# A gated mix of a scan and an MLP on one core: tile 3 of B by transposing loads, a later gate product, half scan tables and carried states on GpSimd

## The chip, the core and the metric

The kernel runs on one core of a Trainium2 chip. The core has TensorE (PE; its weight loads are PEld), VectorE (DVE), ScalarE (ACT), GpSimd (POOL) and SyncE (SP), which here only issues DMAs. Transfers issued from SP and from POOL run on the same 16 DMA engines. The metric is the device time of one execution in microseconds (us), less is better.

## What is computed

```python
g = sigmoid((x * gate_w).sum(-1, keepdims=True))
# a: a diagonal complex recurrence over 2048 tokens, 1024 states
Bu   = einsum("bld,pd->blp", x, B_bar)        # B_bar from B_re, B_im, Lambda, dt
h[t] = Lam_bar * h[t-1] + Bu[t]
a    = 2 * einsum("blp,dp->bld", hseq, C).real + x * Dskip
# b: layer norm, then an MLP of 1024 -> 3584 -> 1024
b    = gelu(layernorm(x) @ w1 + b1) @ w2 + b2
out  = g * a + (1 - g) * b
```

x is 2048 x 1024, all inputs and the output are bfloat16.

## The kernel before

Everything is built as a graph of tasks (`Graph.add`, `Graph.dma`); `schedule` orders the tasks of each engine, and the kernel is then emitted in that order, with semaphore waits where a task needs another engine's result. PE's order is written out by hand (each product depends on the one before it). The order of ACT, DVE, POOL and SP is the planner's: `_latest` goes backwards from PE's order and gives each task a latest start, `_schedule_latest` goes forwards and lets each engine take the ready task with the earliest latest start. For a DMA the planner uses an issue time, a rate and a landing time (constants at the top of the file).

All large products are done in a form that needs seven products for a 2 x 2 block of tiles instead of eight (`SG`, steps p1 to p7; sums of the operands S1..S4, T1..T4 are made by DVE, partial sums are moved by ACT with `seed` and `snap`). One group of it in the first stage is 28 matmuls of 512 columns.

The stages:
- **Opening** (0 to about 28 us). x (rows 0 to 511) and the B rows of tiles 0 to 3 are loaded and transposed by PE (`t_x`, `t_b0`, `t_b`, 8 transposes for each 128 rows), and ACT or DVE copies the result from PSUM. Chunks 1 to 3 of x, 512 rows each, come by transposing loads of 1 MB (`xT_dma`, line 1232, SP). `bu_plain` makes the products of tile 0 with chunks 0 and 1, and the first steps of the groups of tiles 1 and 2 (`early`) stand between.
- **Products of x with B** (to about 112 us). Groups (tile, half of x) in the order (1,0), (2,0), (3,0), (0,1), (1,1), (2,1), (3,1), then tiles 4 to 7. Before p1 of a group, the B rows of its tile must be there with sums S1 to S4 (`b_sums`); T1 to T3 of a half of x are made in `x_sums`, T4 in `x_sum4`, which overwrites the place 2 of that half, where the first half of the odd chunk's transposed x stands. Tiles 4 to 7 come by transposing loads (`bT_dma`, line 1316). The gate product `z_gate` (line 1289: 32 matmuls with two columns of weights, needs all four chunks) stands inside group (2,0), ahead of its p6; its result goes to DRAM and back (`z_move`), and gives the gate and the sums for the layer norm. `ln_stats` squares x on ACT, works out mean and variance in small POOL instructions (lines 1253 to 1258), normalises on DVE and stores to DRAM; transposing loads (line 1468) bring it back for the MLP.
- **Scan tables** (lines 972 to about 1010). Powers of e^(i theta) for 256 positions of all eight tiles are made by doubling, 8 levels of 6 DVE instructions; the last level has 8 x 128 elements in a partition.
- **MLP**, with the scan as filler on DVE: 16 units (`ssm`), each with four products with tables and four combinations, eight scans of 256 positions (line 1426), and three small instructions (fx1, fx2, fx3: lines 1435, 1437, 1439) that turn the last states into the initial states of the next unit. The two temporary tiles MA and MB are shared by all units.
- **Product of the states with C** and the output (from about 451 us).

Of the kernel before, what the change touches and what calls it, by code (L numbers as in the profile page):

```python
# [17 lines left out]
DMA_LAT = 2.0  # L18
# [4 lines left out]
DMAT_BW = 150e3  # L23
OPENING = 12.0
SP_ISSUE = 0.12
ACT_ISSUE = 0.12
POOL_ISSUE = 1.2
# [144 lines left out]
class Graph:  # L172
# [7 lines left out]
    def add(self, eng, dur, prio, emit, reads=(), writes=(), name="", kind="c", nbytes=0, sem=None,  # L180
            xpose=False, extra=(), ndma=1, bw=None, thr=False):
        t = Task()
        t.bw = bw
# [41 lines left out]
    def _schedule_once(self):  # L225
# [27 lines left out]
        while ev:  # L253
# [17 lines left out]
            for e in engs:  # L271
# [25 lines left out]
                if t.kind == "dma":  # L297
                    issue_end = st + t.dur
                    push(issue_end, 1, e)
                    ts = max(issue_end, chan_free[e])  # L300
                    busy_o = sum(1 for o in chan_free if o != e and chan_free[o] > ts)
                    bw_eff = t.bw * (1.0, 0.55, 0.4)[busy_o]
# [78 lines left out]
    def _schedule_latest(self, ls):  # L381
# [57 lines left out]
        while ev:  # L439
# [8 lines left out]
            for e in engs:  # L448
# [13 lines left out]
                if t.kind == "dma":  # L462
                    issued = t.start + t.dur
                    push(issued, 1, e)
                    ts = max(issued, chan_free[e])
                    others = sum(1 for o in chan_free if o != e and chan_free[o] > ts)
                    chan_free[e] = ts + t.nbytes / (t.bw * (1.0, 0.55, 0.4)[others])
# [98 lines left out]
def build(nc, A_x, A_Lambda_re, A_Lambda_im, A_B_re, A_B_im, A_C_re, A_C_im, A_log_dt, A_Dskip,  # L566
# [25 lines left out]
    with es:  # L592
# [105 lines left out]
        for nm in ("DTC", "A", "TH", "R", "PHI", "KFX", "TTR", "T2", "KF2", "T3", "S1", "C1", "UR", "UI",  # L698
                   "Q", "Q2", "INV", "N1", "N2", "N3", "N4", "E20R", "E20I", "SS", "CC", "NMS"):
            alloc_cols(nm, PT)  # L700
# [163 lines left out]
        for pt in range(1, 4):  # L864
            load_b(pt, (-0.85, pt))
# [93 lines left out]
        def tmpd(which, n):  # L959
            return AR.v(TD + which * (PT * T // 2) * 4, [(n, PT), (1, n)], F32)  # L960
# [14 lines left out]
        v = w1(0, 0, 1)  # L975
        g.add("dve", 0.12, PT1, lambda e, v=v: e.memset(v.ap, 1.0), writes=[v], name="e1r0")
        v = w1(1, 0, 1)
        g.add("dve", 0.12, PT1, lambda e, v=v: e.memset(v.ap, 0.0), writes=[v], name="e1i0")
        for k in range(LT):
# [3 lines left out]
            a0, a1, o0, o1, t0, t1 = w1(0, 0, n), w1(1, 0, n), w1(0, n, n), w1(1, n, n), tmpd(0, n), tmpd(1, n)  # L983
# [6 lines left out]
        NTAB = PT * T  # L990
        e1r = AR.v(E1, [(T, PT), (1, T)], F32)
# [161 lines left out]
        def bu_plain(pt, c):  # L1153

            ks = 2
            for ri in range(2):
# [12 lines left out]
        def b_sums(pt, q):  # L1169
            def bv(i, dt=FP16):  # L1170
                return AR.v(bqo(pt, i), [(1, 512)], dt)
            dve_tt("bs1_%d" % pt, q, bv(4), bv(2, BF16), bv(3, BF16), ALU.add, 512)
            dve_tt("bs2_%d" % pt, q, bv(5), bv(4), bv(0, BF16), ALU.subtract, 512)
            dve_tt("bs3_%d" % pt, q, bv(6), bv(0, BF16), bv(2, BF16), ALU.subtract, 512)
# [9 lines left out]
        def x_sum4(pr, q):  # L1184
            xv2, xv1, xv5 = AR.v(xqo(pr, 2), [(1, 2048)], FP16), AR.v(xqo(pr, 1), [(1, 2048)]), AR.v(xqo(pr, 5), [(1, 2048)], FP16)
            dve_tt("ut4_%d" % pr, q, xv2, xv1, xv5, ALU.subtract, 2048)

        def bu_group(pt, pr):
# [8 lines left out]
            mv = {"B11": xl(0, BF16), "B21": xl(1, BF16), "B22": xl(3, BF16), "T1": xl(4), "T2": xl(5), "T3": xl(6), "T4": xl(2)}  # L1197
# [5 lines left out]
            uc = AR.v(SSM + 14336 if bu_n[0] < 7 else TD + 4096, [(1, 512)], F32)  # L1203
# [3 lines left out]
            def fin(qd, q, bk):  # L1207
# [6 lines left out]
                else:  # L1214
                    sv = su if ri == 0 else s5
                    src = sv
                    if ri == 0:
                        g.add("dve", c_dve(CH), (1.0, q - 2), lambda e: e.tensor_tensor(ev.ap, V(PS[bk], 0, [(1, 2 * T)]), src.ap, ALU.add),
                              reads=[b_ps[bk], sv], writes=[ev, b_ps[bk]], name="u" + nm)
# [10 lines left out]
        def xT_dma(c, prio):  # L1230
            o = AR.v(xqo(c // 2, 2 * (c % 2)), [(512, DT), (1, 512)])
            g.dma(prio, lambda e: e.dma_start_transpose(out=o.ap, in_=x2[c * CH:(c + 1) * CH, :]), CH * D * 2,  # L1232
                  ssem("xT", c), writes=[o], name="xT%d" % c, xpose=True, bw=240000.0)
# [79 lines left out]
        def bT_dma(pt):  # L1313
            for ri, ap in enumerate((A_B_re, A_B_im)):
                o = AR.v(bqo(pt, 2 * ri), [(128, DT), (1, 128)])
                g.dma((0.3, pt, ri), lambda e, o=o, ap=ap, pt=pt: e.dma_start_transpose(out=o.ap, in_=ap[pt * 128:(pt + 1) * 128, :]), 128 * D * 2,
                      ssem("bT", 2 * pt + ri), writes=[o], name="bTd%d.%d" % (pt, ri), xpose=True)
# [7 lines left out]
        t_b(3, (1.0, seq[0] + 0.5))  # L1325
        early[1].p2()
        bu_plain(0, 1)
# [8 lines left out]
        for n, (pt, pr) in enumerate(order):  # L1336
# [3 lines left out]
            if (pt, pr) == (0, 1):  # L1340
                x_sums(1, seq[0])
                x_sum4(1, seq[0])
# [8 lines left out]
            if n == 1:  # L1351
                z_gate()
                z_move()
                x_sum4(0, seq[0])
# [35 lines left out]
        def ssm(pg, q):  # L1390
# [37 lines left out]
            if q + 1 < NQ:  # L1428
# [6 lines left out]
                g.add("dve", 0.1, pri(20), lambda e: e.tensor_tensor(V(FXT, 8 * pg, [(2, 4), (1, 2)]), gsw.ap, V(CST, col["KF"] + 8 * pg, [(2, 4), (1, 2)]), ALU.mult),  # L1435
                      reads=[gsw, gfw, bc("KF")], writes=[b_fxt[pg]], name="fx1_" + tag)
                g.add("dve", 0.1, pri(61), lambda e: e.tensor_tensor(V(INIT, 8 * pg, [(2, 4), (1, 2)]), gfw.ap, V(CST, col[CTn] + 4 * pg, [(1, 4), (0, 2)]), ALU.mult),
                      reads=[gsw, gfw, bc(CTn)], writes=bi, name="fx2_" + tag)
                g.add("dve", 0.1, pri(62.5), lambda e: e.tensor_tensor(it, it, fx, ALU.add), reads=bi + [b_fxt[pg]], writes=bi, name="fx3_" + tag)
# [507 lines left out]
```

## Time and profile before

| | us |
|---|---|
| median of three runs | 551.88 |
| the three runs | 555.68, 551.75, 551.88 |
| the profiled execution, its own time | 554.73 |
| its span, first to last instruction | 553.0 |
| PE busy in the span | 546.1 (99%) |
| DVE busy | 510.2 (92%) |
| ACT busy | 287.1 (52%) |
| POOL busy | 89.7 (16%) |

The profile is of one execution. Times in its rows count from the start of the span. A busy PE is a modelled figure, as matmuls overlap; the start of the next row is the better measure of how long a step took.

### The profile page before, as it was taken

The numbers are of one execution on the slowest core, as the hardware profiler recorded it, in microseconds if no ns is written. First come the engines' busy times: TensorE is split into PE (matmuls) and PEld (weight loads), VectorE is DVE, ScalarE is ACT, GpSimd is POOL, SyncE is SP. The second block draws the span as 40 slices with busy tenths as digits, with TensorE's granted clock in tenths as the row PEclk, the third lists the DMA queues.
The fourth block names the chain that finished last, engine by engine and source line by source line (L and its number), as shares of the span: only waits on it lengthen the run. The fifth ranks groups of instructions, "written<-read, shape, count | busy, mean of one in ns | idle before, by whom it ended". The sixth has DMA issues, their size and how long they took to land.

```text
span 553.0 us, 7464 instructions
## 1 busy us (share of the span) xinstructions
PE 546.1 (99%) x2622; PEld 250.2 (45%) x2622; DVE 510.2 (92%) x880; ACT 287.1 (52%) x480; POOL 89.7 (16%) x146
## 2 busy tenths in 40 slices
PE   8899999999999999999999999999999999999997
PEld 5444444444444444444444444444444444444443
DVE  5879989999999999999999999999999999899863
ACT  3767887886773347773347762247672322111110
POOL 0127662540001010001110000220000111001000
PEclk9989999999999999999999999999999999999999
DMA  9996999789762455464666983797767999987531
GB/s 268 252 301 155 272 272 293 252 274 360 237 142 105 164 190 206 148 216 196 225 227 184 310 167 64 135 200 226 240 157 136 230 312 298 376 293 249 180 117 57
DMA packets 115054, 120.07 MB, mean 217 GB/s; under 512 B 70338, under 2 KB 92738, under 8 KB 113994
## 3 DMA queue, kind: packets, MB, share of 16 engines
q1 hardware_dynamic: 102400, 73.69, 47.9%
q0 software_dynamic: 12480, 45.90, 26.8%
q8 instruction: 20, 0.33, 0.2%
q14 instruction: 16, 0.13, 0.1%
q10 hardware_dynamic: 138, 0.02, 0.0%
HBM read 56.40 MB, written 47.46 MB: 188 GB/s over the span
## 4 chain that ended last, share of the span: by engine, by line
PE 94%; SPq 3%; DMA 2%; issue 0%; DVE 0%
PE ps L1034 71%; PE ps L1032 22%; SPq L1232 2%; DMA ar<-in_A_x_dram 2%; PE ps L1289 1%; PE ps L1100 0%; SPq L771 0%; SPq L784 0%; SPq L783 0%; SPq L857 0%; DVE ar L1732 0%
## 5 line engine op out<-in xcount | busy, mean ns | idle before, releaser
L1034 PE MATMUL ps<-ar 128*128 128x512 f16 (+1 forms) x1844 | 416.9, 379 | 0.0
L1034 PEld LDWEIGHTS ps<-ar 128*128 128x128 f16 (+1 forms) x1844 | 180.1, 98 | 218.1 <-issue 1.3
L1032 PE MATMUL ps<-ar 128*128 128x512 bf16 (+1 forms) x608 | 150.0, 379 | 0.0
L1119 DVE TENSOR_TENSOR ar<-ar 128x512 f16<-128x512 bf16 (+7 forms) x224 | 140.0, 662 | 3.9 <-PE ps L1289 2.0
L1032 PEld LDWEIGHTS ps<-ar 128*128 128x128 bf16 (+1 forms) x608 | 59.3, 98 | 71.5 <-ACT ar L833 0.4
L1426 DVE TENSOR_TENSOR_SCAN ar<-cst,init,ar 128x256 bf16<-128x256 f32 x128 | 88.1, 734 | 0.4
L1054 ACT ACTIVATE ar<-ps 128x512 f32<-128x512 f32 x102 | 59.8, 596 | 51.1 <-PE ps L1032 36.8
L1070 ACT ACTIVATE ps<-ps 128x512 f32<-128x512 f32 x67 | 39.0, 582 | 75.4 <-PE ps L1032 64.3
L1412 DVE TENSOR_TENSOR ar<-ar 128x2048 bf16<-128x2048 bf16 x64 | 77.0, 1217 | 0.2 <-ACT ar L1000 0.2
L1533 ACT ACTIVATE ar<-ps,cst 128x512 bf16<-128x512 f32 x56 | 38.4, 686 | 13.4 <-PE ps L1034 13.1
L1055 ACT ACTIVATE ar<-ps,cst 128x512 f32<-128x512 f32 x32 | 22.0, 688 | 44.6 <-PE ps L1034 22.1
L1622 ACT ACTIVATE ar<-ps,cst 128x512 f32<-128x512 f32 x32 | 22.0, 687 | 43.6 <-PE ps L1034 43.6
L1415 DVE TENSOR_TENSOR ar<-ar 128x1024 bf16<-128x1024 bf16 x64 | 42.0, 683 | 0.1
L1539 ACT ACTIVATE ar<-ar,cst 128x512 bf16<-128x512 f32 x56 | 40.0, 713 | 3.7 <-DVE ar L1537 3.5
L1537 DVE TENSOR_TENSOR ar<-ps,ar 128x512 f32<-128x512 f32 x56 | 38.2, 683 | 3.8 <-PE ps L1034 3.1
L1136 POOL DMA_DIRECT2D scr_u<-ar x32 | 24.9, 780 | 44.4 <-ACT ar L1164 20.4
L1745 DVE SCALAR_TENSOR_TENSOR ar<-ps,cst,ar 128x512 bf16<-128x512 f32 x31 | 22.6, 741 | 6.2 <-PE ps L1034 6.0
L1634 POOL DMA_DIRECT2D scr_ac<-ar x16 | 13.8, 892 | 87.5 <-ACT ar L1055 26.1
L1444 POOL DMA_DIRECT2D scr_h<-ar x16 | 9.4, 586 | 108.8 <-DVE ar L1415 88.7
L1625 DVE SCALAR_TENSOR_TENSOR ar<-ps,cst,ar 128x512 f32<-128x512 f32 x32 | 23.6, 741 | 3.5 <-PE ps L1034 2.9
L1632 POOL DMA_DIRECT2D scr_ac<-ar x16 | 8.5, 534 | 83.9 <-DVE ar L1625 54.8
L1716 DVE SCALAR_TENSOR_TENSOR ar<-ar,cst 128x1024 f32<-128x1024 bf16 x16 | 20.1, 1273 | 0.0
(120 smaller groups left out, 248.0 us busy)
## 6 DMA issues: line engine op xcount, KB each, us to landing
scr_ac<-ar POOLq DMA_DIRECT2D x32, 512.0 KB, 5.4
ar<-in_A_x_dram SPq DMA_DIRECT2D x32, 256.0 KB, 5.0
scr_u<-ar POOLq DMA_DIRECT2D x32, 256.0 KB, 5.1
ar<-scr_u SPq DMA_DIRECT2D x16, 512.0 KB, 4.5
scr_h<-ar POOLq DMA_DIRECT2D x16, 512.0 KB, 4.5
ar<-scr_ac SPq DMA_DIRECT2D x16, 512.0 KB, 7.5
ar<-scr_h SPq DMA_DIRECT2D x8, 1024.0 KB, 7.0
ar<-in_B_w_dram SPq DMA_DIRECT2D x14, 512.0 KB, 5.5
```

What stands on the lines that cost most here:

```text
L1032: ins = e.matmul(V(PS[bk], 0, [(1, n)]), st[i].ap, mv[i].ap, start=(i == 0), stop=(i == K - 1))
L1034: ins = e.matmul(V(PS[bk], 0, [(1, n)]), st[i].ap, mv[i].ap, start=False, stop=(i == K - 1), skip_group_check=True)
L1054: return e.activation(o.ap, V(PS[bk], 0, [(1, 512)]), AF.Copy)
L1070: g.add("act", c_act(512), (pb[0], q - 2), lambda e: e.activation(V(PS[b], 0, [(1, 512)]), V(PS[a], 0, [(1, 512)]), AF.Copy), reads=[b_ps[ ...
L1119: g.add("dve", c_tt16(n), (pb[0], q), lambda e: e.tensor_tensor(o.ap, a.ap, b.ap, op), reads=[a, b], writes=[o], name=nm).slack = slack
L1136: g.dma((1.0, q), lambda e: e.dma_start(out=US[pt // 4, :, 4 * pr:4 * pr + 4, r0:r0 + T], in_=evv.ap), 2 * 128 * CH * 2, ssem("us", 2 * ks ...
L1412: g.add("dve", c_tt16(UE), pri(i), lambda e: e.tensor_tensor(o.ap, a.ap, tbl.ap, ALU.mult), reads=[a, tbl], writes=[o], name=nm + tag)
L1415: g.add("dve", c_tt16(UE // 2), pri(i), lambda e: e.tensor_tensor(o.ap, a.ap, b.ap, op), reads=[a, b], writes=[o], name=nm + tag)
L1426: lambda e, pt=pt, ri=ri, vin=vin, go=go: e.tensor_tensor_scan(go.ap, Cb("R", pt, T), vin.ap, V(INIT, pt * 2 + ri, [(1, 1)]), ALU.mult, AL ...
L1533: g.add("act", c_act(512, ap_operands=1), (10.0, q + 1), lambda e: e.activation(o.ap, V(PS[bk], 0, [(1, 512)]), AF.Gelu_apprx_tanh, bias=C ...
L1537: g.add("dve", c_dve(512), (10.0, q - 2), lambda e: e.tensor_tensor(sv.ap, V(PS[bk], 0, [(1, 512)]), sv.ap, ALU.add), reads=[b_ps[bk], sv] ...
L1539: g.add("act", c_act(512, psum=False, ap_operands=1), (10.0, q + 3), lambda e: e.activation(o.ap, sv.ap, AF.Gelu_apprx_tanh, bias=C("B1", ...
```

## The change

Five edits.
- **Tile 3 of B.** It is no longer loaded as rows and transposed by PE: `load_b(3)` and `t_b(3)` go, and `bT_dma(3)` stands ahead of `bT_dma(4)`. `bu_plain(0, 1)` is split: its first half takes the place of `t_b(3)`.
- **Gate product.** `z_gate` and `z_move` go from group (2,0) to group (0,1), two groups later. So that T4 of half 0 doesn't overwrite x before that, it is written to a free place in XN for the first three groups; `x_sum4(1)` follows the gate product. No instruction writes T4 of half 0 to its former place, which the groups of tiles 4 to 7 in half 0 still read, so these read the transposed x there.
- **Half tables.** Doubling makes 128 positions from the middle on (7 levels); ACT mirrors them to the other half (two instructions), DVE copies one column each. The squares of cosine and sine are one instruction instead of two.
- **Carried states.** fx1, fx2 and fx3 go from DVE to POOL. In `fin`, the ACT copy `uc` of the last product of a group goes, and DVE reads PSUM directly.
- **Planner.** Other issue times, rates by name of the load, and a random shift of up to 1 us of the latest start of each task that isn't PE's.

```diff
-DMA_LAT = 2.0
+DMA_LAT = 1.9
+DMA_RATES = {"xT": 240e3, "xnT": 208e3, "ctB": 240e3, "acl": 250e3, "acs": 220e3, "us": 280e3, "xns": 290e3, "hg": 290e3, "ul": 340e3, "w1": 300e3, "w2": 280e3}
-DMAT_BW = 150e3
+DMAT_BW = 180e3
+MIX = (4, 1.0)
-SP_ISSUE = 0.12
+SP_ISSUE = 0.45
-POOL_ISSUE = 1.2
+POOL_ISSUE = 0.8
...
-                    ts = max(issued, chan_free[e])
+                    ts = max(t.start if t.xpose else issued, chan_free[e])
...
+        rng = random.Random(MIX[0])
+        early = {t: MIX[1] * rng.random() for t in self.tasks}
...
-            self._schedule_latest(self._latest())
+            ls = self._latest()
+            for t in self.tasks:
+                if t.eng != "pe":
+                    ls[t] -= early[t]
+            self._schedule_latest(ls)
...
-        for pt in range(1, 4):
+        for pt in range(1, 3):
             load_b(pt, (-0.85, pt))
...
-            dv("ss%d" % k, lambda e, sk=sk: e.tensor_tensor(C("SS", 0, n8), C(sk, 0, n8), C(sk, 0, n8), ALU.mult), [sk], ["SS"])
-            dv("cc%d" % k, lambda e, ck=ck: e.tensor_tensor(C("CC", 0, n8), C(ck, 0, n8), C(ck, 0, n8), ALU.mult), [ck], ["CC"])
+            dv("cs%d" % k, lambda e, ck=ck: e.tensor_tensor(C("CC", 0, 2 * n8), C(ck, 0, 2 * n8), C(ck, 0, 2 * n8), ALU.mult), [ck, sk], ["CC", "SS"])
...
-        for k in range(LT):
+        for k in range(LT - 1):
...
+        for comp, nm, sg in ((0, "MC", 1.0), (1, "MS", -1.0)):
+            src = AR.v(E1 + (comp * NTAB + T - 1) * 4, [(T, PT), (-1, TH - 1)], F32)
+            dst, end = w1(comp, 1, TH - 1), w1(comp, 0, 1)
+            g.add("act", c_act(PT * TH, psum=False), (2.55, comp), lambda e, dst=dst, src=src, sg=sg: e.activation(dst.ap, src.ap, AF.Copy, scale=sg), reads=[src], writes=[dst], name="e1m%d" % comp)
...
-            dve_tt("bs1_%d" % pt, q, bv(4), bv(2, BF16), bv(3, BF16), ALU.add, 512)
+            dve_tt("bs1_%d" % pt, q, bv(4), bv(2, BF16), bv(3, BF16), ALU.add, 512, -2.0 if pt == 3 else 0.0)
...
-                    if ri == 0:
...
-                    else:
-                        g.add("act", c_act(CH), (1.0, q - 2), lambda e: e.activation(uc.ap, V(PS[bk], 0, [(1, 512)]), AF.Copy),
-                              reads=[b_ps[bk]], writes=[uc, b_ps[bk]], name="uc" + nm)
-                        g.add("dve", c_dve(CH), (1.0, q - 2), lambda e: e.tensor_tensor(ev.ap, uc.ap, src.ap, ALU.add),
-                              reads=[uc, sv], writes=[ev], name="u" + nm)
+                    g.add("dve", c_dve(CH), (1.0, q - 2), lambda e: e.tensor_tensor(ev.ap, V(PS[bk], 0, [(1, 2 * T)]), src.ap, ALU.add),
+                          reads=[b_ps[bk], sv], writes=[ev, b_ps[bk]], name="u" + nm)
...
-        t_b(3, (1.0, seq[0] + 0.5))
+        bu_plain(0, 1, (0,))
         early[1].p2()
-        bu_plain(0, 1)
+        bu_plain(0, 1, (1,))
+        bT_dma(3)
         bT_dma(4)
...
-                x_sum4(1, seq[0])
...
             if n == 1:
+                x_sum4(0, seq[0], XN + 24576)
+            if n == 3:
                 z_gate()
                 z_move()
-                x_sum4(0, seq[0])
+                x_sum4(1, seq[0])
...
-                g.add("dve", 0.1, pri(20), lambda e: e.tensor_tensor(V(FXT, 8 * pg, [(2, 4), (1, 2)]), gsw.ap, V(CST, col["KF"] + 8 * pg, [(2, 4), (1, 2)]), ALU.mult),
+                g.add("pool", 0.5, pri(20), lambda e: e.tensor_tensor(V(FXT, 8 * pg, [(2, 4), (1, 2)]), gsw.ap, V(CST, col["KF"] + 8 * pg, [(2, 4), (1, 2)]), ALU.mult),
```

fx2 and fx3 change in the same way as fx1; bs2 and bs3 as bs1.

## Rows read from the trace of the kernel before

**Rows 1.** The page: busy us of each engine, share of the span, instructions

```profile
PE 546.1 (99%) x2622; PEld 250.2 (45%) x2622; DVE 510.2 (92%) x880; ACT 287.1 (52%) x480; POOL 89.7 (16%) x146
```

**Rows 2.** The chain that ended last, in order of time: start, us, what

```profile
19.22 8.73 DMA ar<-in_A_x_dram
28.00 3.22 PE ps L1289 x32
...
547.91 1.76 PE ps L1100 x16
```

**Rows 3.** The longest of PE's waits: who for what, total us, times, longest

```profile
PE ps L1289 <- DMA ar<-in_A_x_dram: 2.2, 1, 2.2
```

**Rows 4.** PE's instructions in order of time: start, us, instruction, idle before

```profile
16.13 1.06 PE L825 MATMUL ps<-ident,ar 128*128 128x128 bf16 x16
17.02 1.03 PE L1034 MATMUL ps<-ar 128*128 128x512 bf16 x4
17.88 4.48 PE L1032 MATMUL ps<-ar 128*128 128x512 bf16 x20
...
31.15 2.22 PE L1034 MATMUL ps<-ar 128*128 128x512 f16 x8
33.20 1.03 PE L1032 MATMUL ps<-ar 128*128 128x512 bf16 x4
...
40.11 1.03 PE L1032 MATMUL ps<-ar 128*128 128x512 bf16 x4
...
112.63 1.03 PE L1032 MATMUL ps<-ar 128*128 128x512 bf16 x4
```

**Rows 5.** Stretches around the gate product: busy by engine, clock, DMA share, GB/s

```profile
25.80:28.00 2.20, 0.02 (x2) 0.00 (x1) 0.60 (x2) 0.60 (x1) 0.14 (x1) 1.00 1.01 374
...
28.40:31.80 3.40, 3.40 (x30) 1.02 (x23) 1.42 (x2) 0.54 (x2) 0.00 (x0) 0.50 1.04 395
```

**Rows 6.** SP's issues in order of time; landing of L784, then of L1232

```profile
6.23 0.45 SPq L784 DMA_DIRECT2D ar<-in_A_B_im_dram  x1
6.72 17.26 SPq L1232 DMA_TRANSPOSE ar<-in_A_x_dram  x3
...
28.85 2.48 SPq L1316 DMA_TRANSPOSE ar<-in_A_B_re_dram  x1
31.38 3.94 SPq L1316 DMA_TRANSPOSE ar<-in_A_B_im_dram  x1
...
DMA to landing us min/median/max: 5.7/6.1/6.5
...
DMA to landing us min/median/max: 7.4/8.7/11.1
```

**Rows 7.** Groups by line: busy, mean ns (POOL and DVE)

```profile
L972 DVE TENSOR_TENSOR ar<-ar,cst 128x1024 f32<-128x1024 f32 x4 | 4.9, 1215 | 0.0
L1437 DVE TENSOR_TENSOR init<-ar,cst 128x8 f32<-128x8 bf16 x14 | 2.2, 159 | 0.0
L1221 ACT ACTIVATE ar<-ps 128x512 f32<-128x512 f32 x15 | 9.0, 597 | 4.1 <-PE ps L1034 3.4 <-DVE ar L1263 0.3 <-DVE ar L972 0.3
L1257 POOL TENSOR_TENSOR cst<-cst 128x4 f32<-128x4 f32 x4 | 4.8, 1196 | 0.1
```

**Rows 8.** DVE from one scan unit to the next, in order of time

```profile
209.27 0.16 DVE L1435 TENSOR_TENSOR fxt<-ar,cst 128x8 f32<-128x8 bf16 x1
...
215.38 1.22 DVE L1412 TENSOR_TENSOR ar<-ar 128x2048 bf16<-128x2048 bf16 x1
...
218.62 2.04 DVE L1426 TENSOR_TENSOR_SCAN ar<-cst,init,ar 128x256 bf16<-128x256 f32 x3
```

**Rows 9.** POOL's longest wait for one store, from the list of waits

```profile
POOL scr_ac L1632 <- DVE ar L1625: 54.8, 7, 29.8
```

**Rows 10.** SP again: the last transposing load of normalised x for the first half

```profile
87.77 5.24 SPq L1468 DMA_TRANSPOSE ar<-scr_xn  x1
...
DMA to landing us min/median/max: 8.7/9.2/9.7
```

More of the change, by code (lines that the diff above doesn't have):

```diff
@@ L1 @@
+import random
 import math
@@ L182, in add @@
         t = Task()
-        t.bw = bw
+        t.bw = DMA_RATES.get(name.rstrip("0123456789.").rstrip("_"), bw)
         t.thr = thr
@@ L299, in _schedule_once @@
                     push(issue_end, 1, e)
-                    ts = max(issue_end, chan_free[e])
+                    ts = max(t.start if t.xpose else issue_end, chan_free[e])
                     busy_o = sum(1 for o in chan_free if o != e and chan_free[o] > ts)
-                    bw_eff = t.bw * (1.0, 0.55, 0.4)[busy_o]
+                    bw_eff = t.bw * (1.0, 0.5, 0.4)[busy_o]
                     chan_free[e] = ts + t.nbytes / bw_eff
@@ L464, in _schedule_latest @@
                     push(issued, 1, e)
-                    ts = max(issued, chan_free[e])
+                    ts = max(t.start if t.xpose else issued, chan_free[e])
                     others = sum(1 for o in chan_free if o != e and chan_free[o] > ts)
-                    chan_free[e] = ts + t.nbytes / (t.bw * (1.0, 0.55, 0.4)[others])
+                    chan_free[e] = ts + t.nbytes / (t.bw * (1.0, 0.5, 0.4)[others])
                     t.finish = chan_free[e] + DMA_LAT
@@ L697, in build @@
         assert ncol[0] == NROW
-        for nm in ("DTC", "A", "TH", "R", "PHI", "KFX", "TTR", "T2", "KF2", "T3", "S1", "C1", "UR", "UI",
-                   "Q", "Q2", "INV", "N1", "N2", "N3", "N4", "E20R", "E20I", "SS", "CC", "NMS"):
+        for nm in ("DTC", "A", "TH", "R", "PHI", "KFX", "TTR", "T2", "KF2", "T3", "C1", "S1", "UR", "UI",
+                   "Q", "Q2", "INV", "N1", "N2", "N3", "N4", "E20R", "E20I", "CC", "SS", "NMS"):
             alloc_cols(nm, PT)
@@ L959, in tmpd @@
         def tmpd(which, n):
-            return AR.v(TD + which * (PT * T // 2) * 4, [(n, PT), (1, n)], F32)
+            return AR.v(TD + which * (PT * T // 4) * 4, [(n, PT), (1, n)], F32)
         def mult_b(name, n):
@@ L974, in build @@
         PT1 = (2.5, 0)
-        v = w1(0, 0, 1)
+        TH = T // 2
+        v = w1(0, TH, 1)
         g.add("dve", 0.12, PT1, lambda e, v=v: e.memset(v.ap, 1.0), writes=[v], name="e1r0")
-        v = w1(1, 0, 1)
+        v = w1(1, TH, 1)
         g.add("dve", 0.12, PT1, lambda e, v=v: e.memset(v.ap, 0.0), writes=[v], name="e1i0")
-        for k in range(LT):
+        for k in range(LT - 1):
             n = 1 << k
@@ L990, in build @@
         NTAB = PT * T
+        for comp, nm, sg in ((0, "MC", 1.0), (1, "MS", -1.0)):
+            src = AR.v(E1 + (comp * NTAB + T - 1) * 4, [(T, PT), (-1, TH - 1)], F32)
+            dst, end = w1(comp, 1, TH - 1), w1(comp, 0, 1)
+            g.add("act", c_act(PT * TH, psum=False), (2.55, comp), lambda e, dst=dst, src=src, sg=sg: e.activation(dst.ap, src.ap, AF.Copy, scale=sg), reads=[src], writes=[dst], name="e1m%d" % comp)
+            g.add("dve", 0.12, (2.55, comp), lambda e, end=end, nm=nm: e.tensor_copy(end.ap, V(CST, col[nm + str(LT - 1)], [(1, PT), (0, 1)])), reads=[bc(nm + str(LT - 1))], writes=[end], name="e1z%d" % comp)
         e1r = AR.v(E1, [(T, PT), (1, T)], F32)
@@ L1151, in mm_half, with bu_plain @@
             return seq[0]
-        def bu_plain(pt, c):
+        def bu_plain(pt, c, ris=(0, 1)):
             ks = 2
-            for ri in range(2):
+            for ri in ris:
                 bk = (4, 5, 6, 1)[2 * c + ri]
@@ L1196, in bu_group @@
             st = {"A11": bl(0, BF16), "A12": bl(1, BF16), "A22": bl(3, BF16), "S1": bl(4), "S2": bl(5), "S3": bl(6), "S4": bl(2)}
-            mv = {"B11": xl(0, BF16), "B21": xl(1, BF16), "B22": xl(3, BF16), "T1": xl(4), "T2": xl(5), "T3": xl(6), "T4": xl(2)}
+            mv = {"B11": xl(0, BF16), "B21": xl(1, BF16), "B22": xl(3, BF16), "T1": xl(4), "T2": xl(5), "T3": xl(6), "T4": xl(2) if bu_n[0] > 2 else [AR.v(XN + 24576 + d * 1024, [(1, 512)], FP16) for d in range(4)]}
             if bu_n[0] % 2:
@@ L1232, in xT_dma @@
             g.dma(prio, lambda e: e.dma_start_transpose(out=o.ap, in_=x2[c * CH:(c + 1) * CH, :]), CH * D * 2,
[L1233 removed]
+                  ssem("xT", c), writes=[o], name="xT%d" % c, xpose=True, bw=200000.0)
         b_xns = [B("xns%d" % k) for k in range(NTT)]
@@ L1434, in ssm @@
                 bi = [b for a in range(4) for b in b_init[4 * pg + a]]
[L1435 removed]
+                g.add("pool", 0.5, pri(20), lambda e: e.tensor_tensor(V(FXT, 8 * pg, [(2, 4), (1, 2)]), gsw.ap, V(CST, col["KF"] + 8 * pg, [(2, 4), (1, 2)]), ALU.mult),
                       reads=[gsw, gfw, bc("KF")], writes=[b_fxt[pg]], name="fx1_" + tag)
[L1437 removed]
+                g.add("pool", 0.5, pri(61), lambda e: e.tensor_tensor(V(INIT, 8 * pg, [(2, 4), (1, 2)]), gfw.ap, V(CST, col[CTn] + 4 * pg, [(1, 4), (0, 2)]), ALU.mult),
                       reads=[gsw, gfw, bc(CTn)], writes=bi, name="fx2_" + tag)
[L1439 removed]
+                g.add("pool", 0.5, pri(62.5), lambda e: e.tensor_tensor(it, it, fx, ALU.add), reads=bi + [b_fxt[pg]], writes=bi, name="fx3_" + tag)
             mul("na", full(so), full(MB), tb(2), 60)
```

17 lines of the change are left out of this document (7 added, 10 removed).

## The prediction

> **What bounds the kernel now.** I read the page first: PE is busy 99% of the span, DVE 92%, ACT 52%, POOL 16% [rows 1]. With PE at that share the question is only where its remaining time lies, so the next view is the chain of waits in order of time. The reader is to see that it is one unbroken run of PE from 28.00 us to the last matmuls at 547.91, and that what stands before 28.00 is a load: the third transposing load of x, issued at 19.22, landed 8.73 later, at 27.95, and the gate product starts on it [rows 2]. The list of PE's waits says the same from the other side: apart from the start, PE waits once in the whole execution, 2.2 us for that load [rows 3]. The stretches around it show a second loss: PE idles from 25.8 to 28.0, 0.4 us later the granted clock goes from 1.00 to 0.50 (from 2.4 to 1.2 GHz), and it stays there for 3.40 us [rows 5].
>
> So DVE, ACT, POOL and the DMA queues are worth nothing directly: no work saved there shortens PE's run, it only widens the cover. Only three things can move the end: PE's instructions, the wait at 25.8 with the slow clock behind it, and new waits.
>
> **The change part by part.** *Gate product later.* It was the only user, at that point, of chunks 2 and 3 of x. In its new place, behind p5 of group (0,1), these chunks are needed anyway. The wait goes: -2.18 us (27.98 less 25.80). The matmuls themselves are the same 32. The slow clock goes if the wait brought it: 3.40 us at half clock do the work of 1.70, so -1.70. Of these 1.38 lie in the gate product (28.40 to 31.15, half of it [rows 4, 5]), which would take 1.77 instead of 3.15 us, and 0.32 in the matmuls behind it. If the clock falls whenever this product runs, the term is 0.
>
> *Tile 3 by transposing loads.* 16 transposes go from PE: 17.02 less 16.13, -0.89 us [rows 4]. ACT loses two copies, SP two plain loads. But the first products with chunk 1 move up into the gap, from 17.88 to 16.13 [rows 4], and chunk 1 landed at 6.72 plus 11.1, 17.8 us [rows 6] (the longest of the three landings must be the first, since the third is the 8.7 of the chain and 17.88 is where PE goes on). It comes earlier, as two plain loads ahead of it are gone: by 0.98 us if SP's issue sets it (two issues of 0.49, from 6.23 to 6.72 [rows 6]), by 1.4 if the bytes do (0.5 MB at the 374 GB/s of [rows 5]). That is 16.4 to 16.8, so a new wait of 0.3 to 0.7 us; behind it on PE stands everything. I take 0.5. Bounds: 0, and 1.7 if the load gains nothing.
>
> The two new transposing loads stand in SP's queue among the others. The planner ranks by latest start; p1 of group (3,0) comes one group before the first use of chunks 2 and 3, so they should be issued behind chunk 1 and ahead of chunks 2 and 3. From 5.74 the first load holds SP for at most 7.5 us, and the pair of this kind that was issued first in the run before held it 2.48 and 3.94 [rows 6], so both are issued by 19.7, some 7 us before p1 of (3,0), which comes at 27.2 (33.20 less the wait, less 3.15 of the gate product ahead of it, less 0.32, less 0.89, plus 0.5 [rows 4]). Chunk 3 then is pushed back by at most 6.4 us: 27.95 less 0.98 plus 6.4, 33.4. Its sum T1 is needed by p5 of (0,1) at 35.8, and takes 1.2 on DVE (the same operation and size in all, 2048 elements of 16 bits, as line 1412 [rows 8]), so it must land by 34.6. Cost 0, with 1.2 us to spare at the worst.
>
> *Later norm.* The gate product now ends at about 38.4 (40.11 for p1 of (0,1), plus three products of 0.86, less the 6.04 gained by then, plus 1.77) instead of 31.15 [rows 4], 7.3 later. The sums of x, the statistics, the normalised rows and their transposing loads hang on it. The last of these for the first half is issued at 87.77 and lands 8.7 to 9.7 later, at 96.5 to 97.5 [rows 10]; 7.3 later is 103.8 to 104.8. The MLP's first product comes at 112.63 less 4.3, 108.4 [rows 4]. Cost 0, with 3.6 to 4.6 us of cover.
>
> *Half tables, squares.* Six DVE instructions of 1.215 us go, 7.3 us [rows 7]; ACT gets two of 1024 elements, about the length of two of its copies there. *Carried states.* 42 instructions of 0.16 us leave DVE, 6.7 us at most [rows 7]. *uc.* 15 ACT copies of 0.597, 9.0 us, go; DVE still makes the same 15 additions, now from PSUM. All of it is off PE's run: 0. The cover: DVE kept up with PE with 92% busy, now has about 14 us less to do, and must do it in 4 us less. What gets worse is that a bank is freed by DVE's addition and no longer by ACT's copy; the bank is written again two groups on, so DVE may be several us late before PE sees it.
>
> On POOL the three small instructions cost more. The nearest rows are its instructions of 128 x 4: up to 1.2 us on average for the slowest line [rows 7], so 3.6 us a unit. Between the end of a unit's scans and the next scan lie 9.35 us (209.27 to 218.62), and 6.1 to the product that overwrites the tile that they read (the second such product, at 215.38) [rows 8]. Bounds: 0, and what a POOL store in front of them would add (below). I take 0. The Trainium skill (GPSIMD Engine Reference, Specifications) states that GpSimd shares its SBUF interfaces with VectorE and contends with DVE instructions that have two SBUF inputs, which is what nearly all the scan's products are; this speaks against the move. If each of the three had to wait out one such product, an estimate by that rule would be 3 x (1.2 + 1.2), 7.2 us: over the 6.1, under the 9.35. No row of this trace tells contention from POOL's own slowness.
>
> *Sum.* -2.18 - 1.70 - 0.89 + 0.5 = -4.27 us on the profiled execution's 554.73: 550.46. The median of the runs is 551.88, 2.85 below that execution, and the third run lies 3.8 above the other two. That spread is about the 3.88 of the wait and the clock together, so the two short runs may well have lost less there. If they lost as much, the new median is 547.6; if what they save is already this wait, it stays at 550.5. I can't tell which, and take the middle: 549.0.
>
> **The rivals.** *The wait comes back in the opening.* If SP takes the loads of tile 3 behind chunks 2 and 3, they are issued at 23.0 (6.72 plus 17.26 less 0.98) and, with the shortest landing of a transposing load there, 7.4, land at 30.4 against 27.2 [rows 6]: 3.2 us of wait, and if the clock falls again 1.7 more. The gain shrinks to 1.1 or turns into a loss of 0.6: 551 to 552.5. For it: the queue is in order, and a random shift is added to the ranks. Against: the shift is at most 1 us, the distance a whole group of 6.
>
> *The clock falls with the gate product.* It fell 0.4 us into it [rows 5], with two columns of weights per matmul, and may fall again in the new place. Then -1.70 isn't had: 550.7 from the middle. Against: it came back with the product hardly over, and the 2.2 us of idleness came first.
>
> *The norm comes late.* If the chain behind the gate product slips by more than the 3.6 to 4.6 us of cover, PE waits at about 108, one us for each. The stores on POOL and the loads on SP are in order, with other loads in between; 3 us too much give 552.
>
> *POOL holds up the scan (the other side).* POOL is in order, and a store there waited up to 29.8 us for the DVE result that it stores [rows 9]. If the planner puts fx1 to fx3 behind such a store, DVE, in order too, stands at the next scan, and behind it stand the additions that free PE's banks. It decides from the point where the three come more than 9.35 us late. One such hold of 20 us leaves DVE idle about 10; PE goes on for a group or so of 6 us and then stands about 5. Two of 16 units so: +10, 559. Against: the planner models POOL's waits, and DVE has 14 us of new slack.
>
> **How the numbers follow.** Forecast 58%, of its own range 547.0 to 551.0; wait back 12%; clock 10%; norm late 10%; POOL 10%. The predicted time is the forecast's, 549.0. The low end is 547.0, the full sum on the median with no new wait; the high end takes in the wait that comes back and the norm by 3 or 4 us, 553.0. About 1% (5.5 us) is what a measurement of this kernel tells from no change. Faster by more needs more than all of the sum, 4.77 with the new wait at 0: 0.06. Slower by more is POOL's rival: 0.10. The rest, 0.84, is within 1%.
>
> **What would show it.** In the profile after: no wait of PE at the gate product, and the product in 1.8 us at clock 1.00; no PE transposes for tile 3, and PE waiting 0.3 to 0.7 us for chunk 1 near 16.1; transposing loads of B issued between chunk 1 and chunk 2; the last load of the normalised first half at about 104; scans that never wait for POOL. The forecast is wrong if PE shows any other wait of over 1 us, above all near 27, near 108, or behind DVE in the MLP; and if PE shows none and the time is still 552, then the short runs before had no such wait.

## The result, and the profile after

The changed kernel takes 555.18 us (median of 22 runs, 552.46 to 560.78) against 551.94 us of the kernel before on the same chips. The ratio is 1.0055, with a 95% interval from 1.0038 to 1.0072: slower by 3.2 us, within 1%, and 2.2 us above the range that was predicted. The mean granted clock parts the runs: it was 0.999 or 1.000 in 72 of the 78 runs of the kernel before that stood beside the experiments, but in only 10 of the 22 of the changed one, and those 10 took 552.46 to 554.85 us, the other 12, at 0.991 to 0.997, 554.86 to 560.78.

One edit bears on every figure here: as tiles 4 to 7 get no T4 of half 0, their product p4 there is not the one that the form asks for. The changed kernel, and every run below that has the edits of the opening, leaves out that sum. It would be one DVE instruction more, an estimate of 1.2 us by the row of T1 below (30.38 us, the same operation and size). No run has it, so what the complete kernel takes is open.

Two traces can now be laid side by side, and a third is needed. The profiled execution of before (554.73 us) stands 2.85 us above the median of its runs, and the prediction could not tell what the usual execution looks like. The last run below is a second trace of the same kernel, at 551.75 us, and is taken here as the usual one: its granted clock is 1.00, as in most runs of before. The table follows PE through three places that are in every trace; all are start times in the span.

| | before, profiled | before, usual | after, profiled |
|---|---|---|---|
| p1 of group (1,1), behind the gate product in all three | 46.15 | 43.06 | 42.33 |
| first matmul of the last stage | 451.27 | 448.18 | 447.45 |
| its last block | 547.75 | 544.65 | 548.23 |
| from the one to the other | 96.48 | 96.47 | 100.78 |
| span | 553.0 | 549.9 | 553.1 |

The gain of the opening is there, and it arrives at the last stage: 3.82 us against the execution that was profiled before, but only 0.73 against the usual one. And the last stage gives back 4.30 us. Against the usual execution: -0.73, +4.31, and -0.38 behind the last block, +3.2 us in the span.

The opening of after, PE in order of time (start, us, instruction, idle before), and SP's issues there:

```profile
37.04 1.90 PE L1296 MATMUL ps<-ar,gwc 128*2 128x512 bf16 x32
```

```profile
5.93 11.85 SPq L1239 DMA_TRANSPOSE ar<-in_A_x_dram  x2
17.89 1.24 SPq L1323 DMA_TRANSPOSE ar<-in_A_B_re_dram  x1
19.23 1.25 SPq L1323 DMA_TRANSPOSE ar<-in_A_B_im_dram  x1
20.53 5.31 SPq L1239 DMA_TRANSPOSE ar<-in_A_x_dram  x1
```

The gate product has no idle time ahead of it and takes 1.90 us, where [rows 2] had 3.22. Tile 3 of B is issued ahead of chunk 3. PE's longest wait has moved to the other end of the kernel (who for what, total us, times, longest); its list has two others, 1.2 us at the start and 1.1 for x rows near 6.7 us:

```profile
PE ps L1046 <- DVE ar L1133: 2.4, 1, 2.4
```

The wait of 2.4 us is in the fourth group of the last stage. PE there, in order of time:

```profile
483.49 1.89 PE L1048 MATMUL ps<-ar 128*128 128x512 f16 x8
487.83 2.88 PE L1046 MATMUL ps<-ar 128*128 128x512 f16 x8 [2.45 <-DVE ar L1133]
```

Behind p7 at 483.49, p5 waits 2.45 us for the sum S1 of the states, and its eight matmuls then take 2.88 us instead of 1.89. The stretch around it (us, busy of PE, PEld, DVE, ACT, POOL, granted clock, DMA share, GB/s), of after and below it of the profiled before:

```profile
480.00:500.00 20.00, 17.55 (x74) 7.45 (x73) 19.90 (x28) 1.78 (x3) 1.67 (x4) 0.91 0.75 239
```

```profile
480.00:500.00 20.00, 20.00 (x94) 9.09 (x93) 20.00 (x28) 2.71 (x5) 1.08 (x2) 1.00 0.84 275
```

In this stretch the clock is at 0.50 from 488.6 to 492.0, 1.7 us of full speed lost, as in [rows 5] right behind PE's idleness; with the wait of 2.45 that is 4.15 of the 4.3 us. The 10 runs at full clock can't have lost the 1.7, so the 4.3 us are those of the profiled execution and not of every run. And the third figure should have been read before the prediction: DVE is busy for 20.00 us of 20 in the kernel before as well. What DVE does ahead of the sums, in after:

```profile
471.30 0.69 DVE L1724 TENSOR_TENSOR ar<-ar 128x1024 bf16<-128x1024 bf16 x1 [3.26 <-DMA ar<-in_A_x_dram]
487.09 1.89 DVE L1133 TENSOR_TENSOR ar<-ar 128x1024 f16<-128x1024 bf16 x3
```

DVE stands 3.26 us for x rows of the output stage (`xd`, the multiplication by the skip weights), then works without a gap, and comes to the sums at 487.09. Counted from PE's first matmul of the stage, PE wants the first sum at 37.77 us, and it takes 0.68. When DVE began it: 35.42 in the profiled before, 35.52 in the usual one, 39.64 in after. Before had 1.6 us to spare there. The usual before, PE's p5 of that group and DVE's first sum:

```profile
485.95 1.89 PE L1032 MATMUL ps<-ar 128*128 128x512 f16 x8
```

```profile
483.70 0.69 DVE L1119 TENSOR_TENSOR ar<-ar 128x1024 f16<-128x1024 bf16 x1
```

The 4.1 us by which the sums come later have two parts. DVE's last wait for x rows ends 23.85 us into the stage in after and 21.85 in the usual before (471.30 and 470.03 us): 2.0. And between that and the sums DVE works for 15.8 us in after and for 13.7 in the usual before: 2.1.

### The profile page after: what moved, and what is told of

The parts are those of the page before. It is cut to its first block, busy times and chain, and to the rows that moved or that the text cites. A ratio compares the mean times of both kernels' runs of the same rounds, so it can differ in the third digit from the quotient of the medians.

```text
span 553.1 us, 7443 instructions
## 1 busy us (share of the span) xinstructions
PE 545.3 (99%) x2606; PEld 249.0 (45%) x2606; DVE 500.3 (90%) x826; ACT 278.1 (50%) x465; POOL 107.4 (19%) x188
## 4 chain that ended last, share of the span: by engine, by line
PE 91%; DMA 4%; DVE 4%; issue 1%; SPq 0%; DVEq 0%
PE ps L1048 68%; PE ps L1046 22%; DMA ar<-in_A_x_dram 4%; DVE ar L1133 1%; DVE ar L1725 1%; DVE ar L1754 1%; DVE ar L1724 0%; DVE ar L1752 0%; PE ps L1296 0%; PE ps L834 0%; PE ps L1114 0%; PE ps L1161 0%; PE ps L810 0%; SPq L780 0%; DVE ar L1634 0%
## 5 line engine op out<-in xcount | busy, mean ns | idle before, releaser
L1133 DVE TENSOR_TENSOR ar<-ar 128x512 f16<-128x512 bf16 (+7 forms) x224 | 142.4, 663 | 1.5 <-DMA ar<-in_A_x_dram 1.1
L1444 POOL TENSOR_TENSOR fxt<-ar,cst 128x8 f32<-128x8 bf16 x14 | 9.8, 696 | 136.3 <-DVE ar L1435 136.3
L1230 DVE TENSOR_TENSOR ar<-ps,ar 128x512 bf16<-128x512 f32 x30 | 20.6, 688 | 9.4 <-PE ps L1048 9.3
L1643 POOL DMA_DIRECT2D scr_ac<-ar x16 | 13.8, 881 | 38.5 <-DVE ar L1634 22.1
```

The lines of the kernel that those rows point to most:

```text
L1133: g.add("dve", c_tt16(n), (pb[0], q), lambda e: e.tensor_tensor(o.ap, a.ap, b.ap, op), reads=[a, b], writes=[o], name=nm).slack = slack
```

## The experiments

Times are medians; ratios are against the kernel before, run on the same chip in between (551.5 to 551.8 us). "Sums at" is the start of DVE's first sum of that fourth group, counted from the first matmul of the stage; PE wants it at 37.8, so up to 37.1 is in time (later where PE had waited in the stage already: 0.9 us in "opening alone", 1.0 in "old planner").

| | us | ratio, 95% | PE at last stage | sums at | stage |
|---|---|---|---|---|---|
| after | 555.18 | 1.0055 [1.0038, 1.0072] | 447.45 | 39.64 | 100.78 |
| PE delayed | 553.58 | 1.0044 [1.0027, 1.0062] | 450.49 | 35.83 | 96.47 |
| short x loads | 552.01 | 0.9999 [0.9985, 1.0014] | 448.26 | 36.99 | 96.48 |
| short xd | 552.40 | 1.0008 [0.9990, 1.0027] | 448.07 | 36.72 | 96.47 |
| four sums first | 550.69 | 0.9982 [0.9967, 0.9997] | 448.39 | 35.17 | 96.50 |
| the same, bank freed first | 550.15 | 0.9966 [0.9949, 0.9984] | 447.19 | 35.07 | 96.48 |
| xd later | 550.50 | 0.9962 [0.9921, 1.0003] | 447.26 | 35.72 | 96.48 |
| old planner | 551.94 | 0.9984 [0.9951, 1.0017] | 447.13 | 38.65 | 98.11 |
| old planner, xd later | 550.62 | 0.9954 [0.9923, 0.9986] | 447.58 | 31.92 | 96.48 |
| opening alone | 555.04 | 1.0036 [1.0002, 1.0070] | 451.49 | 37.35 | 97.55 |
| opening, half tables | 552.23 | 1.0013 [1.0001, 1.0025] | 449.05 | 35.31 | 96.47 |

For "PE delayed" the stage is counted from behind the added matmuls.

**Is it the order of the four sums?** In the cleanest run every engine keeps the order of the changed kernel, and only the four sums move up in DVE's queue, ahead of the `xd` at 482.46 us and the five instructions behind it:

```diff
...
+        for nms, dst in ((('ys1_3', 'ys3_3', 'ys2_3', 'ys4_3'), 'xd15'),):
+            ts = [dve.pop(at(nm)) for nm in nms]
+            i = at(dst)
+            dve[i:i] = ts
```

> The changed kernel with the planner's order kept on every engine, but for one thing: in DVE's queue the four sums of the fourth group of the last stage (S1 to S4) stand five instructions earlier, ahead of the multiplication of x rows at 482.46 us. No instruction is added, dropped or changed. Theory (the 4.3 us that the last stage loses are PE's wait for these sums and the clock that falls with it, and nothing else): the last stage takes 96.5 us from its first matmul to its last block instead of 100.8, no wait of PE there, no half clock at 480 to 500, about 550.9 us (549.9 to 551.9). Rival (DVE is simply full there: whatever is moved ahead pushes another instruction that PE needs back by the same 2.4 us): PE waits 1 to 2.5 us for a later addition, 553.5 or more. Rival (traffic of the loads slows the stage): unchanged, 555.

Measured 550.69 us, the stage 96.50 us, clock 1.00:

```profile
483.56 2.61 DVE L1139 TENSOR_TENSOR ar<-ar 128x1024 f16<-128x1024 bf16 x4
```

```profile
480.00:500.00 20.00, 19.95 (x94) 8.94 (x94) 19.86 (x27) 2.36 (x4) 1.16 (x3) 1.00 0.76 272
```

No work was added or taken away, DVE is as full as before (19.86 of 20), and it still waits for x rows, 3.41 us. So neither a full DVE nor the loads alone cost the 4.3 us of the stage: the place of the sums in DVE's queue did, with them. What was pushed back by the four sums is nothing that PE wants soon. PE comes to the stage 0.94 us later than in after, but the result doesn't hang on that: the first sum is ready at 484.24, and in after PE wanted it at 485.2.

**Does an earlier PE alone do it?** Rather than bring DVE forward, the next run holds PE back: the first product of the stage is made three times over.

```diff
...
+                for i in (list(range(K)) * 2 if nm == "p1_y0" else []): e.matmul(V(PS[bk], 0, [(1, n)]), st[i].ap, mv[i].ap, start=(i == 0), stop=(i == K - 1))
```

> The changed kernel with the 8 matmuls of the first product of the last stage made three times: PE comes 3.45 us later into that stage, and the order on every other engine and queue is the same. Theory 1 (the last stage is paced by loads and by DVE; PE comes 3.8 us earlier and waits there): the wait of 2.4 us and the slow clock behind it (1.7 us) go, the time changes by -1 to +0.5 us. Theory 2 (the loads and DVE follow PE, and the wait lies in their new order): the wait stays and the time is 3.4 us longer.

553.58 us: 3.45 us of work more for PE, and not slower than the changed kernel (ratio 1.0044 against 1.0055, in overlapping intervals; the medians lie 1.6 us apart, a little more than the -1 that was expected at most). Apart from the start PE waits for nothing, and the clock is 1.00 throughout. DVE's first sum begins at 486.32 us, 0.8 earlier than in after, though PE comes 3.0 later. Two more runs make DVE's way to the sums shorter and leave every order as it is: the x row loads of the last stage cut to 64 of 1024 columns, and the sixteen `xd` multiplications cut to 64 columns.

```diff
+ ... e.dma_start(out=AR.v(XV[xi], [(1, 64)]).ap, in_=x2[k * 128:(k + 1) * 128, 0:64]) ...
```

> The changed kernel with the 16 loads of x rows in the last stage cut to 64 of 1024 columns (so the skip term is wrong there), order unchanged: 3.9 MB less, about 11 us of the queue at 338 GB/s. Theory 1, with the loads as the pace: DVE's wait for x rows near 468 to 471 us goes, and with it PE's wait: -3 to -4 us. If DVE's own work is the pace (it is busy over 90% there): -1 to 0 us, PE still waits for DVE's sums.

```diff
+ ... e.tensor_tensor(AR.v(XV[xi], [(1, 64)]).ap, AR.v(XV[xi], [(1, 64)]).ap, AR.v(DB, [(1, 64)]).ap, ALU.mult) ...
```

> The changed kernel with DVE's 16 multiplications of x with the skip weights in the last stage on 64 of 1024 columns (skip term wrong there), order and loads unchanged: 0.55 us less each, about 2.8 us less between 471 and 487 us. Theory 1: DVE still waits for the x rows near 471, but its sums for the fourth group are ready about 2.8 us earlier: PE's wait goes nearly, -3 to -4 us with the clock. If the wait were for a load alone: 0.

552.01 and 552.40 us; by the ratios 3.1 and 2.6 us less than the changed kernel, the second just short of what was expected. Both stages take 96.5 us. With the short loads DVE waits 0.60 us for x rows instead of 3.26; with the short multiplications it still waits 2.76, and the sums are in time all the same. So the load and the multiplications both make the sums late. That either one alone would cure it is not shown: the sums begin 1.84 and 2.30 us earlier in the span than in after, less than the 2.45 us of PE's wait, and the rest is that PE comes to the stage 0.8 and 0.6 us later in these two traces, by a wait in the opening that is shown below.

Another engine for the multiplications, GpSimd:

```diff
-                g.add("dve", c_tt16(D), (52.0, n), lambda e, xv=xv: e ...
+                g.add("pool", 2.0, (52.0, n), lambda e, xv=xv: e ...
```

> The changed kernel with those 16 multiplications moved to GpSimd, everything computed; the planner makes a new order. Theory 1: DVE has 11 us less in the last stage, PE's wait there goes, 550 to 552 us, if GpSimd takes less than about 2 us for each. Theory 2: the order decides, anything from 550 to 560.

567.93 us, ratio 1.029 [1.0269, 1.0310], above what either theory gave. One multiplication takes GpSimd 2.13 us (median) against 0.68 on DVE, DVE waits for it, 8.0 us in all, and PE three times for later sums (3.57, 3.78 and 1.01 us). The new order also costs 4.6 us ahead of the stage, where PE waits 2.58 us at 283 for an addition of DVE; so this run shows that GpSimd is no cure in this order, and not in every one. The first of the three waits:

```profile
494.15 3.51 PE L1046 MATMUL ps<-ar 128*128 128x512 f16 x8 [3.57 <-DVE ar L1133]
```

**A second wait, in the opening.** Three of the runs with the order kept (short x loads, short xd, four sums first) showed one more thing, which the profiled execution of after and the run with PE delayed don't have. PE and DVE of the run with the sums first:

```profile
32.70 2.77 PE L1054 MATMUL ps<-ar 128*128 128x512 f16 x11 [0.95 <-DVE ar L1236]
```

```profile
30.38 1.23 DVE L1139 TENSOR_TENSOR ar<-ar 128x2048 f16<-128x2048 bf16 x1 [1.73 <-DMA ar<-in_A_x_dram]
31.96 0.68 DVE L1236 TENSOR_TENSOR ar<-ps,ar 128x512 bf16<-128x512 f32 x1
```

L1236 is the addition that frees the bank of p7 of group (2,0) (L1230 in after; before, ACT's copy `uc` freed it). It stands behind the sum T1 that waits for chunk 3, and p4 of the same group writes that bank again after only two products, 1.73 us. So part of the old wait for chunk 3 comes back through DVE and the bank. The next run moves that addition ahead of T1 as well:

```diff
-        for nms, dst in ((('ys1_3', 'ys3_3', 'ys2_3', 'ys4_3'), 'xd15'),):
+        for nms, dst in ((('ys1_3', 'ys3_3', 'ys2_3', 'ys4_3'), 'xd15'), (('u2.1.1',), 'ut1_1')):
```

> As the run before, and in the opening the addition that frees the bank of p7 of group (2,0) stands ahead of the sum that waits for chunk 3. Theory (the freed bank is held up by a sum that waits for a load, in part of the executions, by up to 1.3 us): never a wait of PE at about 32 us, PE is at the last stage at 447.0 to 447.5, and the time is 0 to 1.2 us below the run before: 549.7 to 550.9. Rival (the sum T1 of chunk 3 comes late instead, for p5 of group (0,1)): PE waits there at about 36 us, time as the run before or above it.

550.15 us, PE at the last stage at 447.19 and no wait behind the start: the list of PE's waits has one line, that of the start. At a ratio of 0.9966 [0.9949, 0.9984] this version, as the run before it, is faster than both kernels; the 0.5 us between the two runs lie inside their intervals, and that the wait is gone is shown by one trace.

**Planner or operations?** The old planner with the other edits of the change:

```diff
...
-DMA_RATES = {"xT": 240e3, ...}
-MIX = (4, 1.0)
-SP_ISSUE = 0.45
+SP_ISSUE = 0.12
-                ls[t] -= early[t]
...
```

> The changed kernel with the planner's constants, rates and transposing start as before, and without the random shift: the edits of the operations alone. The order of that planner puts DVE's sums for the fourth group of the last stage further ahead of the product that needs them. Theory 1: the x rows still land near 470, the wait for those sums is shorter than 2.4 us; 550 to 552. Theory 2: no wait in the last stage, 547.5 to 549.5. If the operations themselves cost time (POOL's three, the missing copy): 553 or more.

And both planners with a planned reserve of 8 us on `xd` (so that it ranks later; this shifts ranks elsewhere too):

```diff
+ ... name="xd%d" % k, extra=pe_last if yi > 2 else ()).slack = 8.0
```

> As the run with the old planner, and the planner takes the x rows of the last stage to be 8 us later than it thinks (slack of the multiplication that reads them), so that DVE's sums for PE come ahead of work that waits for these rows. Theory 1: PE's wait in the last stage goes, 548.5 to 550.5, faster than both kernels. If the loads alone set PE's pace, no change against the old planner's run.

> The changed kernel with that slack of 8 us alone. Theory 1: DVE's order in the last stage fits the true landing, the wait of 2.4 us and the slow clock go or shrink to under 1 us: 550 to 553, 2 to 4 us better than the changed kernel. If the wait is not one of order: 555.

551.94, 550.62 and 550.50 us; the second is 0.1 above what was expected. With the old planner PE waits twice in the stage, first for an addition that frees a bank, then for the sums:

```profile
480.89 1.90 PE L1039 MATMUL ps<-ar 128*128 128x512 f16 x8 [1.00 <-DVE ar L1745]
486.52 1.90 PE L1037 MATMUL ps<-ar 128*128 128x512 f16 x8 [0.28 <-DVE ar L1124]
```

The stage loses 1.6 us (98.11 against 96.48), and the four edits of operations together come out where the kernel before is, 0.9984 [0.9951, 1.0017]. The other 2.7 us of the stage, the longer wait and the clock that falls with it, come with the new planner; which of its settings (issue times, rates, the random shift) makes that order was not taken apart, and another seed of the shift was not tried. With `xd` ranked later the stage takes 96.48 us under either planner, and the two runs don't differ: once that order is mended, no run shows the new settings to gain or cost anything.

**The opening alone.** Only the later gate product and the loads of tile 3, on the kernel before:

```diff
-        for pt in range(1, 4):
+        for pt in range(1, 3):
...
-        t_b(3, (1.0, seq[0] + 0.5))
+        bu_plain(0, 1, (0,))
...
+        bT_dma(3)
...
+            if n == 3:
                 z_gate()
...
```

> The kernel before with the edits of the opening alone (tile 3 by transposing loads, gate product two groups later, T4 of half 0 beside; as in the changed kernel, tiles 4 to 7 then read transposed x in its place). Theory 1 (whatever the opening gains, the last stage takes): PE comes to the last stage about 3.5 us earlier than the 451.3 of the profile before, and waits there for DVE's sums of the fourth group; 551 to 553 us. Theory 2 (the new order alone spoils the last stage): the opening's gain stays, 547.5 to 549.5.

555.04 us, outside both theories: PE is 1.05 us ahead of the usual before at 42.01 us, but 3.3 us behind it at the last stage, where it then waits 0.90 us for an addition and not for the sums. In between it waits five times, 0.23, 0.52, 1.35, 0.61 and 0.42 us, for two copies of ACT, a sum of DVE, a load of weights and an addition of DVE. The longest:

```profile
113.68 3.63 PE L1034 MATMUL ps<-ar 128*128 128x512 f16 x15 [1.35 <-DVE ar L1119]
```

With these waits, five steps from one group to the next, 6.04 us otherwise, are 6.44, 6.74, 7.56, 6.82 and 6.95: 4.3 us lost. At 111.51 DVE normalises rows (L1263) just ahead of the sum for which PE waits longest: there the norm comes late, as one of the rivals had it, but not over its loads, over DVE. Half tables and joined squares added to it, nothing else:

```diff
...
+            dv("cs%d" % k, ...)
...
-        for k in range(LT):
+        for k in range(LT - 1):
...
+        for comp, nm, sg in ((0, "MC", 1.0), (1, "MS", -1.0)):
...
```

> The kernel before with the opening edits (tile 3 by transposing loads, later gate product) and the half tables with the joined squares; copies in ACT, carried states on DVE and the planner are those of before. Theory (with the opening edits alone, 555.0 us, PE gave the gain back in five waits of 3.1 us together between 81 and 142 us, because DVE still had 7.3 us more of table work there): these waits are gone or under 0.8 us together, PE is at the last stage at 447 to 448.5 instead of 451.5, and the time is 551.0 to 553.0, the last stage's own wait of about 1 us included. Rival (the waits come from the ACT copy that frees the bank and from loads): 2 us or more of waits stay, 554 or more.

552.23 us. The waits fall to 0.3 and 1.1 us, the loss on the way to 1.9 us instead of 4.3. They did not fall under 0.8 together as expected, and PE comes to the last stage at 449.05, not by 448.5; the rest goes with the other operation edits (with all of them PE comes there at 447.13 with the old planner and at 447.45 with the new one). So the work saved on DVE was not worth nothing: with the tables alone 2.4 us of PE's time came back once the gate product came later. Each of these runs has an order of its own, so the 2.4 are those of the shorter work and of its order together.

**The kernel before once more,** with no edit:

> The kernel before, unchanged, for a second trace of it. Its profiled execution was 2.85 us above the median of the others, and only there the mean granted clock was under 1.00. Theory: in the usual execution PE waits for the third transposing load of x all the same, 1 to 2.2 us ahead of the gate product, but the granted clock stays at 1.00, so the usual execution lost 1 to 2.2 us there and not 3.9. Rival (the usual execution has no such wait, and the change had nothing to win in the opening but the 16 transposes): wait under 0.5 us.

The rival holds. PE, and the landing of the three transposing loads of x (us from issue, min, median, max):

```profile
26.54 1.90 PE L1289 MATMUL ps<-ar,gwc 128*2 128x512 bf16 x32
```

```profile
DMA to landing us min/median/max: 7.2/7.3/10.8
```

The third load, issued at 19.13 (19.22 in [rows 2]), lands in 7.2 us instead of 8.73; PE comes 0.74 us later, having waited 0.9 us for x rows between 6 and 8 us. The gate product starts without a wait of PE, at full clock. But its first weight load waited 0.42 us for that load, to 26.54: it came just in time, and the two traces of this kernel lie on either side.

## Why the prediction was wrong, step by step

From 551.88 the forecast went down by 2.9 us, and the time went up by 3.2. Two steps failed. The larger is the cover: the prediction put all that changes on DVE at 0, with a mean of 92% as its reason, and gave the planner's edit no term; in its place the last stage lost 4.3 us in the trace. The smaller is the term of -3.88 for the wait and the slow clock at the gate product, of which the forecast, as the middle, still counted about 2.5; in the usual execution there was nothing of it to win.

- **The wait and the clock at the gate product, -3.88.** The mechanism was right: after, the product has no wait and takes 1.90 us, and with the transposes 3.82 of the 4.27 us arrive at the last stage. But they were won from an execution that was not the usual one. What failed is the middle between 547.6 and 550.5: an execution as short as the two short runs (551.75 us) had neither the wait nor the slow clock, which the prediction named as a possibility, and for the opening the upper figure was the right one. From the usual execution only the transposes were to be had: 0.89 was forecast, 0.73 came in after and 0.99 in the run with the sums and the bank first.
- **A new wait for chunk 1, +0.5.** Not seen: the products with it go on at 16.00 without idle time. PE had waited 1.1 us for an x row tile, up to 6.66, which the profiled before did not; the usual before had lost 0.9 us there too.
- **Loads of tile 3.** The cost of 0 was right: issued by 20.5 (19.7 at the latest was forecast), no wait at p1 of (3,0). The order was not: they stand behind chunk 2, not ahead of it, and each holds SP for 1.25 us, less than the 2.5 to 3.9 of [rows 6].
- **"Worth nothing directly", and 92% as cover.** Wrong, and the main error. A mean of 92% hides a stretch of 100%; there DVE was 1.6 us ahead of PE, and it came 4.1 us later on the stage's own clock, so PE waited 2.45 us and the clock fell. Moving the four sums up, with nothing else changed, took the stage from 100.78 to 96.50 us. The prediction looked for the loss where the edits were (the opening, the norm, the scan) and had no rival for the last stage, where no operation was edited and only the order moved. It met the planner's random shift in one place alone, with the remark that 1 us is small against a group of 6; against a margin of 1.6 us it was not compared.
- **"The bank is written again two groups on".** Wrong for p7: two products on, by p4 of the same group. It cost 0.95 to 1.3 us in the runs where chunk 3 came late.
- **The norm.** The cost of 0 was right for the change as a whole, the reckoning was not: the last load of the first half was not 7.3 us later, about 95, but was issued at 87.3, as before (87.77), and landed by 96.1, not at about 104. The opening alone shows that the cover was made by the table edits, which the sum had put at 0: its waits of 3.1 us fell to 1.4 with the shorter tables.
- **GpSimd.** The rival with 10% did not come: DVE waited for GpSimd 0.7 us in all, and that for the norm, not for one of the three instructions. The bound that the prediction took from the slowest line, 3.6 us a unit, is what the longest unit took. The rows of one unit, POOL's and then DVE's:

```profile
208.86 1.24 POOL L1444 TENSOR_TENSOR fxt<-ar,cst 128x8 f32<-128x8 bf16 x1 [10.28 <-DVE ar L1435]
210.06 1.18 POOL L1446 TENSOR_TENSOR init<-ar,cst 128x8 f32<-128x8 bf16 x1
211.32 0.20 POOL L1448 TENSOR_TENSOR init<-init,fxt 128x8 f32<-128x8 f32 x1
```

```profile
208.81 2.36 DVE L1421 TENSOR_TENSOR ar<-ar 128x2048 bf16<-128x2048 bf16 x2
211.10 0.68 DVE L1546 TENSOR_TENSOR ar<-ps,ar 128x512 f32<-128x512 f32 x1
```

The first two last as long as one DVE product each, the third, beside an addition from PSUM, 0.20 us. The longest of the fourteen units takes 3.6 us for the three, under the 6.1 and 9.35 us that the prediction read for a unit.

What stays open: why the first x rows for which DVE waits in the last stage land 23.8 us after its start in after and 20.2 in the usual before (and the second ones there 21.9). The new planner issues them in another order and the DMA engines are full there (share 1.02 and 1.03), but the two were not taken apart. Open too are which of the planner's settings made the order, and the time with T4 of half 0 in its place.

## What to carry to other kernels

When one engine is the whole path, look at the others in windows, not by their mean: where a second engine is at 100%, read how long ahead of its use each of its results is ready, and price every change of order against that margin. Before a wait is put into a sum, see whether the usual execution has it; a profiled run that stands above the median may have lost its time just there. And an edit that only widens cover is worth what the other edits take from that cover.

## What the runs showed of the hardware

- A small GpSimd instruction (128 x 8) took 0.19 to 0.21 us (once 0.50) beside a DVE addition that reads PSUM. Issued during a DVE instruction with two SBUF inputs it ended with it, as in the rows above, so it took up to 1.25 us, and once 3.20, across four such instructions with nothing between them. The other way round, with the multiplications on GpSimd, a DVE instruction of 1.27 us took up to 3.29. The Trainium skill (SBUF — State Buffer, Summary: rules for kernel authors) says that of a DVE instruction with two SBUF inputs and a GpSimd one that reads SBUF, the second to issue waits until the first is done. These rows agree. The 7.2 us that the prediction estimated was about twice the longest unit.
- The granted clock went from 1.00 to 0.50 (2.4 to 1.2 GHz) after 2.2 us of PE idleness in [rows 5], after 2.45 us in after, and after 2.58, 3.57 and 3.78 us with the multiplications on GpSimd. In the other traces, with waits of 0.2 to 1.35 us, its mean stayed at 1.00.
- The third transposing load of x, 1 MB, landed in 7.2 us in one execution of the kernel before and in 8.73 in another.
